# Where a recurrent-memory transformer kernel computes and stores its early values, and how its light and last steps are ordered

## The chip, the cores and the metric

The kernel runs on one core of one Trainium2 chip. The metric is the device time of one execution in microseconds (us). A time shown for a kernel is the median of several executions; a profile is one execution, recorded by the hardware, and its span runs from the first instruction to the last.

A core has five engines with a queue each. TensorE (PE) multiplies matrices, VectorE (DVE), ScalarE (ACT) and GpSimd (POOL) work on elements, and SyncE (SP) computes nothing: here it issues nearly all DMA transfers, one behind the other. An engine works through its own queue in order and waits at an instruction until the semaphores that this instruction needs have been raised.

## What is computed

Four layers are run in turn on a sequence of 2048 tokens of width 512: an attention layer A with a recurrent memory, a dense layer B, then A and B again with the same weights.

```python
def _A_ref(x, mem0, Wq, Wk, Wv, Wo, seg_len):        # seg_len 32, M 8 memory rows, H 32 heads of 128
    mem = mem0
    for s in range(n_seg):                            # 64 segments
        xs = x[:, s * seg_len:(s + 1) * seg_len, :]
        h = concatenate([mem, xs], axis=1)            # 40 rows
        q, k, v = h @ Wq, h @ Wk, h @ Wv              # per head
        p = softmax(where(mask, q k^T * scale, -1e9))
        o = (p @ v) @ Wo
        mem = o[:, :M, :]                             # goes into the next segment
        outs.append(o[:, M:, :])
def _B_ref(x, w1, w2):                                # 512 -> 1376 -> 512
    return relu(x @ w1) @ w2
x = x + _A_ref(layernorm(x), mem0, ...)
x = x + _B_ref(layernorm(x), w1, w2)
x = x + _A_ref(layernorm(x), mem0, ...)
x = x + _B_ref(layernorm(x), w1, w2)
```

Each segment needs the memory that the segment before it produced, so the segments of one layer can't run side by side.

## The kernel before

**Steps.** Time is cut into 68 steps, k = 0 to LAST = 67. Step k works on segment k of the first attention layer and on segment k-4 of the second one, so steps 0 to 3 and 64 to 67 hold one attention layer ("single") and the 60 between them hold two. The chain inside a step is: queries and keys of 16 heads (`qk`, matmuls in `qk_batch`, L528), `scores` (L562), `softmax`, the same for the other 16 heads, transposed probabilities (`transpose_p`, L604), `weighted_v` (L630), `output_mem` (L570) for the memory rows, `new_memory` (L763, casts at L757, L774, L777), and `memory_values` (L711), the values of the new memory rows. The rest is put between as filler for PE: the outputs of the step before (`block`, `output_x`, L364/L387/L392), the dense layer (`dense_h`, L464; `dense_y`, L487), values of the second layer (L345) and values of the first layer that don't hang on the memory (`values0`, L304).

**Order.** For PE, DVE, SP and POOL the order in which the code is written is the order of the queue. ACT's order is chosen by the scheduler when the program is built.

**Values of the first layer.** A group is `values0(p, n)`: the 64 tokens of segments 2p and 2p+1 times 1024 columns of Wv, eight 128x512 matmuls; ACT casts the result into an SBUF buffer, and two DMAs store it into a DRAM tile `vd0[p]`, from which the step that needs it loads its rows (`load_values`). Only odd p go this way, four groups each. Step 0 computes eight groups, step 1 four, and then every fourth step, 5, 9, ..., up to 61, a few (`values_at`): three in steps 5 to 33, four in steps 37 to 61. A step with three is called light (`split`), and so is step 1; in it the dense layer's first product comes after the second scores, in a step with four before them.

**Buffers.** In step 0 the cast values stand in the space of w1 and w2 (`slots`), which are loaded only in step 1 (`load_dense`). Later they stand in one of five buffers named `vst`, which the values of the memory (`VmS`) and a copy of the new memory (`wm`) use too.

**Loading and SP's queue.** At the start SP issues the loads of Wq, Wk, Wv (two halves each) and Wo (four pieces, L148), 16 MB in all, then the stores of step 0 as their casts come, then in step 1: the load of 128 rows of x (`load_xb`), the values of segment 1 (L685), the two stores of the memory's values (L716), their two loads (L721), w1 and w2 in three DMAs (L156, L157, L159), and the stores of step 1's groups (L312). Step 2 follows on the same queue: stores of its memory values, `Vs` of segment 2 (L693), the transpose of the normalized rows by DMA (`transpose_step`, L287, into `xnT`, which `dense_h` reads), the loads L721 and the transpose of the probabilities (L611). SP's DMAs take eight semaphores in turn, so each DMA also waits until the DMA eight places earlier has landed.

**Inputs.** `xbs[n]` holds 128 rows of x, which are normalized and transposed into `xT0[n]` (`inputs_T`): by PE for n < 3, by DMA from n = 3 on, in step 3 for n = 3. Groups with p = 2n and 2n+1 read it.

**The last step.** Step 67 divides the outputs of step 66 over its waits in pieces of 8, 8 and 16 heads (`part`, `block`). Behind it stand `output_x(LAST)`, whose products are summed in two halves by head (`by_heads`), the sums into the residual (`add_output`, L408), a layer norm, a transpose and the last dense layer.

Of the kernel before, what the change touches and what calls it, by code (L numbers as in the profile page):

```python
# [7 lines left out]
BF = mybir.dt.bfloat16  # L8
# [14 lines left out]
def kernel(  # L23
# [14 lines left out]
    nc = tc.nc  # L38
# [92 lines left out]
    hh = H // 4  # L131
# [102 lines left out]
    def transpose_pe(xn):  # L234
        tp = ps_fill.tile([128, NC4, 128], BF, tag="fill", name="tpx")
        for c4 in range(NC4):
            nc.tensor.transpose(tp[:, c4, :], xn[:, c4 * 128:(c4 + 1) * 128], ident[:])
        return tp

    def inputs_T(n):  # L240
        xT0[n] = wk.tile([128, NC4, 128], BF, tag="xT0", bufs=3, name="xT0")
        if n < 3:
            tp = transpose_pe(xbs.pop(n))
            nc.scalar.copy(out=xT0[n][:], in_=tp[:])
        else:
            nc.sync.dma_start_transpose(out=xT0[n][:], in_=xbs.pop(n)[:])

# [41 lines left out]

    def values0(p, n, lo=0, hi=NC4, pool=None, stage=None):
        r = 64 * (p % 2)
        if (n, lo) == (0, 0):
            vd0[p] = dram.tile([64, H * Dh], BF, tag="vd0", bufs=3, name="vd0")
        if lo == 0:
            pool, tag = (pool, "wo") if pool else (ps_fill, "fill")
            vp_tiles[p, n] = pool.tile([128, 512], F32, tag=tag, name="vp")  # L300
        vp = vp_tiles[p, n]
        for c4 in range(lo, hi):
            for j in range(2):
                nc.tensor.matmul(vp[64 * j:64 * j + 64, :], lhsT=xT0[p // 2][:, c4, r:r + 64],  # L304
                                 rhs=Wv_sb[:, c4, (n + j) * 512:(n + j + 1) * 512],
                                 start=(c4 == 0), stop=(c4 == NC4 - 1), tile_position=(0, 64 * j))
        if hi < NC4:
            return
        vst = wk.tile([128, 512], BF, tag="vst", bufs=5, name="vst")[:] if stage is None else stage
        nc.scalar.copy(out=vst, in_=vp[:])  # L310
        for j in range(2):
            nc.sync.dma_start(out=vd0[p][:, (n + j) * 512:(n + j + 1) * 512], in_=vst[64 * j:64 * j + 64, :])  # L312

    def values_first(ii):

# [130 lines left out]

    def dense_h(d):
        if not 0 <= d <= LAST:  # L450
            return
        lo, hi = span(d)
        n = hi - lo

        def cols(c4):
            return xnT_tiles[d + 2][:, c4, lo:hi]

        hT = hT_tiles[d] = wk.tile([128, NFC, 64], BF, tag="hT", bufs=1, name="hT")
        for f0, f1 in ((8, NFC), (0, 4), (4, 8)) if d == LAST - 1 else ((8, NFC), (0, 8)):
            hp = ps_fill.tile([128, 8, 64], F32, tag="fill", name="hp")  # L460
            for fc in range(f0, f1):
                fs = 128 if fc < NFC - 1 else F_LAST
                for c4 in range(NC4):
                    nc.tensor.matmul(hp[0:fs, fc - f0, 0:n], lhsT=w1_sb[:, c4, fc * 128:fc * 128 + fs],  # L464
                                     rhs=cols(c4), start=(c4 == 0), stop=(c4 == NC4 - 1))
# [236 lines left out]
    def memory_values(k, stage=(None, None), part=range(2)):  # L702
        if 0 in part:
            vmds[k] = dram.tile([2, 4, 32, 512], BF, tag="vmd", bufs=7, name="vmd")
        vmd = vmds[k]
        for ii in part:
            vp = ps_c.tile([128, 512], F32, tag="c", name="vm")
            for c4 in range(NC4):
                for j in range(4):
                    n = 4 * ii + j  # L710
                    nc.tensor.matmul(vp[32 * j:32 * j + 32, :], lhsT=HTm[:, c4, :],  # L711
                                     rhs=Wv_sb[:, c4, n * 512:(n + 1) * 512],
                                     start=(c4 == 0), stop=(c4 == NC4 - 1), tile_position=(0, 32 * j))
            VmS = wk.tile([128, 512], BF, tag="vst", bufs=5, name="VmS")[:] if stage[ii] is None else stage[ii]
            nc.scalar.copy(out=VmS, in_=vp[:])  # L715
            nc.sync.dma_start(out=vmd[ii].rearrange("j t e -> (j t) e"), in_=VmS)  # L716

    def load_memory_values(k, act):
        for ii in range(2):
# [6 lines left out]
    def block(k, lo, hi):  # L726
        output_x(k - 1, lo, hi)
        groups = values_at(k)
        if split(k):

            rest = [(i, 0, NC4) for i in range(1, len(groups))]
            todo = [(0, 0, 2)] if lo == 0 else [(0, 2, NC4)] if hi == 16 else rest
        else:
            todo = [(i, c4, c4 + 2) for i in range(len(groups)) for c4 in range(0, NC4, 2)
                    if lo < 8 * i + 2 * c4 + 2 <= hi]
        for i, c_lo, c_hi in todo:
            p, n = groups[i]
            values0(p, n, c_lo, c_hi, ps_wo if i in (0, 2 if len(groups) == 3 else 3) else None)

    def split(k):  # L740
        return k == 1 or len(values_at(k)) == 3

    def values_at(k):


        if k == 1:
            return [(5, 4), (5, 6), (3, 4), (3, 6)]
        if k % 4 != 1 or not has0(k + 1):
            return []
        groups = [(p, n) for p in range(7, NSEG // 2, 2) for n in range(0, NCH, 2)]  # L750
        i = k // 4 - 1
        lo = 3 * min(i, 8) + 4 * max(i - 8, 0)
        return groups[lo:lo + (3 if i < 8 else 4)]

# [35 lines left out]
    def first_step():  # L790


        slots = iter([w1_flat[:, 512 * i:512 * i + 512] for i in range(NC4 * Dff // 512)] +
                     [w2_flat[:, 512 * i:512 * i + 512] for i in range(4)])
        masks(0)
        with tc.high_priority(offset=PRIO):
            qks = qk(0, [0])
# [34 lines left out]
    def step(k):  # L832
# [68 lines left out]
        if k == 1:  # L901
            normalize(nc.vector, xbs[n_x], xbs[n_x], moments_x(n_x), 0, 128)
        if single and k < LAST and ahead:
            add_dense(k - 2)
            store(k - 2)
# [31 lines left out]
    with tc.manual_schedule(engines={mybir.EngineType.PE, mybir.EngineType.DVE, mybir.EngineType.SP,  # L937
# [79 lines left out]
```

## Time and profile before

| | |
|---|---|
| median of 3 executions | 1606.83 us (1605.47 to 1611.45) |
| the profiled execution, its own time | 1606.83 us |
| its span | 1605.1 us |
| PE busy | 1568.9 us, 98% of the span, 42714 instructions |
| DVE busy | 1264.7 us, 79% |
| ACT busy | 738.8 us, 46% |
| POOL busy | 346.6 us, 22% |
| mean granted TensorE clock | 0.996 |
| DMA traffic of SP's queue | 136.10 MB, 37.9% of 16 engines' span |

The profile names lines as L12, tiles as out<-in, and has several views. A timeline row is: start, duration, engine, line, operation, tiles, size, count, and in square brackets the idle time of the engine just before with what ended it. SPq is SP's queue: the time that it took to issue a DMA, not the time of the transfer. A row of the windows view gives the length of a stretch, busy time and instruction count of each engine, PEclk (the clock that was granted to TensorE, 1.00 is full), the mean busy share of the DMA engines, and GB/s.

### The profile page before, as it was taken

How to read it: one execution, taken by the hardware profiler on the slowest of the kernel's cores; microseconds unless marked ns; L12 is line 12 of the kernel's file. 1: busy time of each engine (PE TensorE's matmuls, PEld its weight loads, DVE VectorE, ACT ScalarE, POOL GpSimd, SP SyncE). 2: the span in 40 equal slices, each digit the busy share in tenths (PEclk: the TensorE clock that was granted, in tenths of full speed). 3: DMA queues.
4: the chain of work that ended last, by engine and by line, in shares of the span. 5: the costliest groups of instructions: out<-in, count | busy, mean ns of one | idle time of the engine just before them, and what ended most of it. 6: DMA issues, size and time to landing. Idle time of an engine off the chain costs nothing.

```text
span 1605.1 us, 94862 instructions
## 1 busy us (share of the span) xinstructions
PE 1568.9 (98%) x42714; PEld 1322.8 (82%) x42714; DVE 1264.7 (79%) x3112; ACT 738.8 (46%) x1799; POOL 346.6 (22%) x666
## 2 busy tenths in 40 slices
PE   5899999999999999999999999999999999999997
PEld 3577888888888888889888887988888898888876
DVE  4478888888888887888888888888888888787865
ACT  3334445444544544454454445445454544545432
POOL 2012222222222222222222222222222222221210
PEclk9999999999999999999999999999999999999999
DMA  9733343343343434434443443343343333334222
GB/s 369 222 83 77 75 87 89 64 97 85 78 76 90 87 63 97 84 72 83 84 92 63 100 85 74 84 84 91 68 100 82 77 77 79 92 61 100 69 70 36
DMA packets 216373, 146.39 MB, mean 91 GB/s; under 512 B 124984, under 2 KB 209312, under 8 KB 214944
## 3 DMA queue, kind: packets, MB, share of 16 engines
q1 hardware_dynamic: 212816, 136.10, 37.9%
q8 instruction: 335, 5.49, 1.5%
q0 software_dynamic: 3072, 4.20, 1.1%
q14 instruction: 70, 0.57, 0.1%
q10 hardware_dynamic: 80, 0.03, 0.0%
HBM read 65.41 MB, written 45.35 MB: 69 GB/s over the span
## 4 chain that ended last, share of the span: by engine, by line
PE 91%; DVE 4%; SPq 2%; issue 1%; DMA 1%; ACT 1%; POOLq 0%; POOL 0%; ACTq 0%; DVEq 0%
PE qp L528 35%; PE wox L364 10%; PE wo L570 8%; PE vm L711 7%; PE v L345 7%; PE hp L464 6%; PE sp L487 5%; PE sp L562 4%; PE pv L630 4%; PE vp L304 3%; SPq L148 1%; PE tp L604 1%; PE xp L438 1%; DMA Wo_sb<-in_A_Wo_dram 1%; SPq L134 1%
## 5 line engine op out<-in xcount | busy, mean ns | idle before, releaser
L534 ACT CAST QT<-qp 128x480 bf16<-128x480 f32 (+3 forms) x408 | 201.1, 493 | 396.0 <-PE qp L528 395.6
L528 PE MATMUL qp<-HT,Wk_sb 128*128 128x80 bf16 (+1 forms) x8704 | 369.7, 200 | 2.7 <-issue 0.9
L528 PE MATMUL qp<-HT,Wq_sb 128*128 128x80 bf16 (+1 forms) x8704 | 370.4, 200 | 1.8 <-POOL HT L700 1.2
L528 PEld LDWEIGHTS <-Wq_sb 128*128 128x128 bf16 x8704 | 326.6, 100 | 33.6 <-issue 26.3
L528 PEld LDWEIGHTS <-Wk_sb 128*128 128x128 bf16 x8704 | 329.0, 100 | 4.5 <-issue 2.9
L536 DVE CAST KT<-qp 128x480 bf16<-128x480 f32 (+3 forms) x408 | 225.1, 565 | 104.1 <-PE qp L528 101.8
L594 POOL TENSOR_TENSOR P_sb<-es,sm 128x320 bf16<-128x320 f32 x185 | 130.5, 719 | 752.9 <-ACT es L584 491.6
L578 DVE TENSOR_REDUCE mx<-sp 128x8 f32<-128x320 f32 x256 | 115.7, 487 | 75.1 <-PE sp L562 73.4
L364 PE MATMUL wox<-Wo_sb,OTx 128*64 128x256 bf16 x2880 | 173.9, 273 | 0.1
L364 PEld LDWEIGHTS <-OTx 128*64 128x64 bf16 x2880 | 150.2, 110 | 3.2 <-issue 0.2
L589 DVE TENSOR_REDUCE sm<-es 128x8 f32<-128x320 f32 x256 | 118.6, 463 | 42.3 <-ACT es L584 32.8
L711 PE MATMUL vm<-Wv_sb,HTm 128*32 128x512 bf16 x2176 | 136.4, 380 | 0.8 <-DVE HT L777 0.8
L584 ACT ACTIVATE es<-es 128x320 f32<-128x320 f32 x256 | 110.2, 469 | 54.2 <-DVE es L582 52.9
L570 PE MATMUL wo<-Wo_sb,OTm 128*32 128x512 bf16 x2144 | 128.7, 381 | 3.4 <-DMA Wo_sb<-in_A_Wo_dram 3.3
L345 PE MATMUL v<-Wv_sb,xnT 128*32 128x512 bf16 x2048 | 129.2, 378 | 0.0
L554 DVE CAST sp<-maskb 128x320 f32<-128x320 bf16 x256 | 118.3, 484 | 0.0
L582 DVE TENSOR_TENSOR es<-sp,mx 128x320 f32<-128x320 f32 x256 | 113.7, 483 | 1.6
L711 PEld LDWEIGHTS <-HTm 128*32 128x32 bf16 x2176 | 89.5, 96 | 28.9 <-issue 11.5
L487 PE MATMUL sp<-w_sb,hT 128*64 128x256 bf16 (+4 forms) x1474 | 105.3, 276 | 0.5 <-ACT hT L470 0.5
L715 ACT CAST VmS<-vm 128x512 bf16<-128x512 f32 x134 | 78.4, 585 | 54.4 <-PE vm L711 54.4
L464 PE MATMUL hp<-xnT,w_sb 128*128 128x64 bf16 (+3 forms) x2948 | 100.5, 193 | 0.5 <-ACT xnT L973 0.4
L464 PEld LDWEIGHTS <-w_sb 128*128 128x128 bf16 (+1 forms) x2948 | 94.3, 101 | 1.5 <-issue 1.1
(113 smaller groups left out, 2027.2 us busy)
## 6 DMA issues: line engine op xcount, KB each, us to landing
Vs<-vd SPq DMA_DIRECT2D x96, 256.0 KB
vmd<-VmS SPq DMA_DIRECT2D x134, 128.0 KB
vd<-vst SPq DMA_DIRECT2D x128, 128.0 KB
Vs<-vmd SPq DMA_DIRECT2D x254, 32.0 KB
Vs<-vmd SPq DMA_DIRECT2D x60, 128.0 KB
vd<-vst SPq DMA_DIRECT2D x112, 64.0 KB
Wq_sb<-in_A_Wq_dram SPq DMA_DIRECT2D x2, 2048.0 KB
Wk_sb<-in_A_Wk_dram SPq DMA_DIRECT2D x2, 2048.0 KB
```

The costliest lines, as they stand in the source:

```text
L345: nc.tensor.matmul(vp[32 * j:32 * j + 32, :], lhsT=tokens[:, c4, :], rhs=Wv_sb[:, c4, n * 512:(n + 1) * 512], start=(c4 == 0), stop=(c4 == ...
L364: nc.tensor.matmul(out[64 * j:64 * j + nr, 0:256], lhsT=lhsT, rhs=rhs[:, 256 * j:256 * j + 256], start=start, stop=stop, tile_position=(0, ...
L464: nc.tensor.matmul(hp[0:fs, fc - f0, 0:n], lhsT=w1_sb[:, c4, fc * 128:fc * 128 + fs], rhs=cols(c4), start=(c4 == 0), stop=(c4 == NC4 - 1))
L487: nc.tensor.matmul(sp_banks[bank][64 * j:64 * j + n, 0:w], lhsT=hT_tiles[d][0:fs, fc, 0:n], rhs=w2_flat[0:fs, fc * Dm + 256 * j:fc * Dm + ...
L528: nc.tensor.matmul(qp[:, hi, 0:ncol], lhsT=W_sb[:, c4, h * Dh:(h + 1) * Dh], rhs=HT[:, c4, a_lo:a_hi, :], start=(c4 == 0), stop=(c4 == NC4 ...
L534: nc.scalar.copy(out=dst[:, 0:nh, a_lo * L:a_hi * L], in_=qp[:, 0:nh, 0:ncol])
L536: nc.vector.tensor_copy(out=dst[:, 0:nh, a_lo * L:a_hi * L], in_=qp[:, 0:nh, 0:ncol])
L554: nc.vector.tensor_copy(out=sp_tiles[a], in_=maskb2)
L570: nc.tensor.matmul(wo[32 * j:32 * j + 32, :], lhsT=OTm[:, h, n, 2 * M * c:2 * M * c + 4 * M], rhs=Wo_sb[:, h, :], start=(h < 4), stop=(h > ...
L589: nc.vector.tensor_reduce(out=sm[:], in_=es[:], axis=AX.X, op=ALU.add)
L594: eng.tensor_tensor(out=P, in0=es[:], in1=sm[:].unsqueeze(2).to_broadcast([128, 8, L]), op=ALU.mult)
L711: nc.tensor.matmul(vp[32 * j:32 * j + 32, :], lhsT=HTm[:, c4, :], rhs=Wv_sb[:, c4, n * 512:(n + 1) * 512], start=(c4 == 0), stop=(c4 == NC ...
```

## The change

Six things are changed.

1. Step 0 computes eleven groups instead of eight (also (3, 4), (3, 6) and (5, 4)), between five pieces of Wo instead of four: 8, 8, 8, 4 and 4 heads. Step 1 has three groups instead of four, step 5 two instead of three, step 37 three instead of four; all other steps keep their number, with the groups moved up.
2. The stores of step 0 that come from `values0` and `memory_values` are not issued in step 0. They are kept in a list (`held`) and issued in step 1 behind `load_memory_values`, ahead of `load_dense`: 24 DMAs. The two stores of `values_second` stay where they were.
3. Rows 384 to 511 of x (n = 3) are loaded behind Wo into a `vst` buffer, which they keep until step 3, normalized in step 1 behind the first batch of queries and keys (before: near the end of step 1), and transposed by PE into an extra copy in the buffer `ob`, from which step 1 computes (7, 0) and (7, 2). The transpose by DMA in step 3 stays.
4. In light steps the first of `dense_h`'s two pieces (12 of 44 matmuls) goes ahead of the second scores. Steps with two or three groups are light; so step 37 becomes light, and 61 and the others with four do not.
5. The last step divides the outputs of step 66 into 4, 4 and 24 heads and puts that same piece of `dense_h` ahead of the last 24.
6. `output_x(LAST)` is summed by quarters of 128 columns instead of two halves of 256 columns by head: 128 matmuls instead of 64, and four sums of 32x128 instead of 32x256.

```diff
 def load_xb(n):
-        tag, bufs = ("vst", 5) if n in (1, 2) else ("xb", 1)
+        tag, bufs = ("vst", 5) if n in (1, 2, 3) else ("xb", 1)
...
+    WO_PARTS = ((0, 8), (8, 16), (16, 24), (24, 28), (28, 32))
...
-        for pc in range(4):
-            nc.sync.dma_start(out=Wo_sb[:, pc * hh:(pc + 1) * hh, :], in_=Wo_v[:, pc * hh:(pc + 1) * hh, :])
+        for h0, h1 in WO_PARTS:
+            nc.sync.dma_start(out=Wo_sb[:, h0:h1, :], in_=Wo_v[:, h0:h1, :])
+        load_xb(3)
...
-    def inputs_T(n):
-        xT0[n] = wk.tile([128, NC4, 128], BF, tag="xT0", bufs=3, name="xT0")
-        if n < 3:
-            tp = transpose_pe(xbs.pop(n))
+    def inputs_T(n, early=False):
+        tag, bufs = ("ob", 1) if early else ("xT0", 3)
+        xT0[n] = wk.tile([128, NC4, 128], BF, tag=tag, bufs=bufs, name="xT0")
+        if n < 3 or early:
+            tp = transpose_pe(xbs[n])
...
+    held = []
+
+    def put(later, **store):
+        if later:
+            held.append(store)
+        else:
+            nc.sync.dma_start(**store)
...
         for j in range(2):
-            nc.sync.dma_start(out=vd0[p][:, (n + j) * 512:(n + j + 1) * 512], in_=vst[64 * j:64 * j + 64, :])
+            put(stage is not None, out=vd0[p][:, (n + j) * 512:(n + j + 1) * 512], in_=vst[64 * j:64 * j + 64, :])
...
     def by_heads(k):
-        return k == LAST or k + 1 < LAST and len(layers(k + 1)) == 1
+        return k + 1 < LAST and len(layers(k + 1)) == 1
...
-    def dense_h(d):
+    def dense_h(d, parts=slice(None)):
...
+        pieces = ((8, NFC), (0, 4), (4, 8)) if d == LAST - 1 else ((8, NFC), (0, 8))
+        for f0, f1 in pieces[parts]:
...
-            nc.sync.dma_start(out=vmd[ii].rearrange("j t e -> (j t) e"), in_=VmS)
+            put(k == 0, out=vmd[ii].rearrange("j t e -> (j t) e"), in_=VmS)
...
     def split(k):
-        return k == 1 or len(values_at(k)) == 3
+        return len(values_at(k)) in (2, 3)
...
-        if k == 1:
-            return [(5, 4), (5, 6), (3, 4), (3, 6)]
+        if k in (1, 5):
+            return [(5, 6), (7, 0), (7, 2)] if k == 1 else [(7, 4), (7, 6)]
...
             wo = ps_wo.tile([128, Dm], F32, tag="wo", name="wo")
-            for i in range(4):
-                if i < 2:
-                    values0(1, 4 + 2 * i, stage=next(slots))
-                output_mem(0, wo, 8 * i, 8 * i + 8)
+            for groups, heads in zip((((1, 4),), ((1, 6),), ((3, 4),), ((3, 6), (5, 4)), ()), WO_PARTS):
+                for p, n in groups:
+                    values0(p, n, stage=next(slots))
+                output_mem(0, wo, *heads)
...
-        if has_x and (k % 4 == 0 or k == 1):
+        if k % 4 == 0 and has_x:
             load_xb(n_x)
         with tc.high_priority(offset=PRIO):
-            qks = qk(0, act, behind=norm_rows.pop(k, None))
+            behind = norm_rows.pop(k, None)
+            if k == 1:
+                def behind():
+                    normalize(nc.vector, xbs[n_x], xbs[n_x], moments_x(n_x), 0, 128)
+            qks = qk(0, act, behind=behind)
             load_values(k, act)
             if k == 1:
                 memory_values(k)
-        part = 8 if single else 5
+                inputs_T(n_x, True)
+        part = 4 if k == LAST else 8 if single else 5
+        mid = 8 if k == LAST else 16
...
             load_memory_values(k, act)
+            while held:
+                put(False, **held.pop(0))
             scores(qks, act)
...
         if single:
-            block(k, part, 16)
+            block(k, part, mid)
         elif light:
+            dense_h(k - 2, slice(0, 1))
             block(k, part, 16)
...
         if single:
-            if k < LAST:
-                dense_h(k - 2)
-            block(k, 16, H)
+            dense_h(k - 2, slice(0, 1) if k == LAST else slice(None))
+            block(k, mid, H)
         elif light:
-            dense_h(k - 2)
+            dense_h(k - 2, slice(1, None))
             block(k, 16, H)
...
         output_x(LAST, 0, H)
-        dense_h(LAST - 2)
+        dense_h(LAST - 2, slice(1, None))
         add_output(LAST)
```

More of the change, by code (lines that the diff above doesn't have):

```diff
@@ L130 @@
     PW = H * Dh // 2
-    hh = H // 4
+    WO_PARTS = ((0, 8), (8, 16), (16, 24), (24, 28), (28, 32))
     def load_w(W_sb, W_v, pc):
@@ L238, in transpose_pe @@
         return tp
-    def inputs_T(n):
-        xT0[n] = wk.tile([128, NC4, 128], BF, tag="xT0", bufs=3, name="xT0")
-        if n < 3:
-            tp = transpose_pe(xbs.pop(n))
+    def inputs_T(n, early=False):
[3 more added lines that the diff above has]
+            tp = transpose_pe(xbs[n])
             nc.scalar.copy(out=xT0[n][:], in_=tp[:])
         else:
-            nc.sync.dma_start_transpose(out=xT0[n][:], in_=xbs.pop(n)[:])
+            nc.sync.dma_start_transpose(out=xT0[n][:], in_=xbs[n][:])
     def norm_parts(k):
@@ L456, in cols @@
             return xnT_tiles[d + 2][:, c4, lo:hi]
-        hT = hT_tiles[d] = wk.tile([128, NFC, 64], BF, tag="hT", bufs=1, name="hT")
-        for f0, f1 in ((8, NFC), (0, 4), (4, 8)) if d == LAST - 1 else ((8, NFC), (0, 8)):
+        if not parts.start:
+            hT_tiles[d] = wk.tile([128, NFC, 64], BF, tag="hT", bufs=1, name="hT")
+        hT = hT_tiles[d]
+        pieces = ((8, NFC), (0, 4), (4, 8)) if d == LAST - 1 else ((8, NFC), (0, 8))
+        for f0, f1 in pieces[parts]:
             hp = ps_fill.tile([128, 8, 64], F32, tag="fill", name="hp")
@@ L731, in block @@
             rest = [(i, 0, NC4) for i in range(1, len(groups))]
-            todo = [(0, 0, 2)] if lo == 0 else [(0, 2, NC4)] if hi == 16 else rest
+            if k == 1:
+                todo = [] if lo == 0 else [(0, 0, 2)] if hi == 16 else [(0, 2, NC4)] + rest
+            else:
+                todo = [(0, 0, 2)] if lo == 0 else [(0, 2, NC4)] if hi == 16 else rest
         else:
@@ L737, in block @@
             p, n = groups[i]
-            values0(p, n, c_lo, c_hi, ps_wo if i in (0, 2 if len(groups) == 3 else 3) else None)
+            values0(p, n, c_lo, c_hi, ps_wo if i in (0, 3 if len(groups) == 4 else 2) else None)
     def split(k):
-        return k == 1 or len(values_at(k)) == 3
+        return len(values_at(k)) in (2, 3)
     def values_at(k):
-        if k == 1:
-            return [(5, 4), (5, 6), (3, 4), (3, 6)]
+        if k in (1, 5):
+            return [(5, 6), (7, 0), (7, 2)] if k == 1 else [(7, 4), (7, 6)]
         if k % 4 != 1 or not has0(k + 1):
             return []
-        groups = [(p, n) for p in range(7, NSEG // 2, 2) for n in range(0, NCH, 2)]
-        i = k // 4 - 1
+        groups = [(p, n) for p in range(9, NSEG // 2, 2) for n in range(0, NCH, 2)]
+        i = k // 4 - 2
         lo = 3 * min(i, 8) + 4 * max(i - 8, 0)
@@ L793, in first_step @@
         slots = iter([w1_flat[:, 512 * i:512 * i + 512] for i in range(NC4 * Dff // 512)] +
-                     [w2_flat[:, 512 * i:512 * i + 512] for i in range(4)])
+                     [w2_flat[:, 512 * i:512 * i + 512] for i in range(8)])
         masks(0)
@@ L839, in step @@
         ahead = has1(k + 1) or not cont
-        if has_x and (k % 4 == 0 or k == 1):
+        if k % 4 == 0 and has_x:
             load_xb(n_x)
         with tc.high_priority(offset=PRIO):
-            qks = qk(0, act, behind=norm_rows.pop(k, None))
+            behind = norm_rows.pop(k, None)
+            if k == 1:
+                def behind():
+                    normalize(nc.vector, xbs[n_x], xbs[n_x], moments_x(n_x), 0, 128)
+            qks = qk(0, act, behind=behind)
             load_values(k, act)
@@ L900, in step @@
             outputs(k, pvs)
-        if k == 1:
-            normalize(nc.vector, xbs[n_x], xbs[n_x], moments_x(n_x), 0, 128)
         if single and k < LAST and ahead:
```

## The prediction

> **What bounds the kernel now.** I read the chain of work that ended last first, then PE's timeline step by step, then SP's queue around steps 0 to 2, then the granted clock. The chain is PE's:
>
> ```profile
> PE 91%; DVE 4%; SPq 2%; issue 1%; DMA 1%; ACT 1%; POOLq 0%; POOL 0%; ACTq 0%; DVEq 0%
> ```
>
> A matmul removed from a full step therefore saves its time, and a late PE is late to the end, because each step needs the memory of the step before. What is left to win lies where PE waits: step 0 (the loads of Wo), a short wait in each light step, and the last step. PE's timeline shows the three.
>
> ```profile
> 49.76 0.79 PE L570 MATMUL wo<-Wo_sb,OTm 128*32 128x512 bf16 x8 [2.15 <-DMA Wo_sb<-in_A_Wo_dram]
> ...
> 82.24 1.34 PE L464 MATMUL hp<-xnT,w_sb 128*128 128x32 bf16 x44
> ...
> 239.23 0.42 PE L562 MATMUL sp<-KT,QT 128*40 128x40 bf16 x16
> 239.83 0.37 PE L562 MATMUL sp<-KT,QT 128*40 128x40 bf16 x16 [0.18 <-DVE sp L554]
> 240.14 1.52 PE L464 MATMUL hp<-xnT,w_sb 128*128 128x64 bf16 x44
> ...
> 1587.92 0.48 PE L604 MATMUL tp<-ident,P_sb 128*64 128x80 bf16 x16 [1.60 <-DVE P_sb L594]
> ...
> 1589.45 3.59 PE L387 MATMUL wox<-Wo_sb,OTx 128*32 128x256 bf16 x64
> ```
>
> The reader should see that the last quarter of Wo's products waits 2.15 us, and that 82.24 is where step 2 first needs w1 and `xnT`: no wait stands before it. The windows view adds the clock:
>
> ```profile
> 47.00:50.00 3.00, 0.85 (x16) 0.33 (x15) 0.00 (x0) 0.00 (x0) 0.00 (x0) 1.00 0.83 274
> 50.00:53.00 3.00, 2.21 (x54) 1.16 (x47) 1.20 (x3) 0.77 (x2) 0.00 (x0) 0.51 0.39 98
> ...
> 1586.10:1589.50 3.40, 1.69 (x70) 1.36 (x60) 2.62 (x7) 1.23 (x3) 0.00 (x0) 1.00 0.00 0
> 1589.50:1592.90 3.40, 3.40 (x64) 2.38 (x64) 1.34 (x5) 0.14 (x1) 0.00 (x0) 0.50 0.02 5
> ```
>
> After each of the two thinly used stretches TensorE is granted half its clock. Last, SP's queue, which I take to decide this change:
>
> ```profile
> 44.31 10.59 SPq L312 DMA_DIRECT2D vd<-w_sb  x12
> ...
> 56.13 2.83 SPq L312 DMA_DIRECT2D vd<-w_sb  x4
> ...
> 60.20 0.89 SPq L716 DMA_DIRECT2D vmd<-VmS  x2
> 63.08 0.67 SPq L721 DMA_DIRECT2D Vs<-vmd  x2
> 63.80 0.40 SPq L156 DMA_DIRECT2D w_sb<-in_B_w_dram  x1
> ...
> 67.40 9.24 SPq L312 DMA_DIRECT2D vd<-vst  x8
> 76.77 1.01 SPq L716 DMA_DIRECT2D vmd<-VmS  x2
> 78.29 0.33 SPq L693 DMA_DIRECT2D Vs<-vd  x1
> 78.73 2.21 SPq L287 DMA_TRANSPOSE xnT<-XN  x1
> ```
>
> Issuing the stores costs SP 0.88 us each while Wo still loads, 0.71 after it (2.83/4). From w1's issue at 63.80 to the product that needs `xnT` at 82.24 the queue has no slack: the transpose is issued until 80.94 and lands near 82.2.
>
> **Step 0 and the start of step 1.** The three added groups fill the waits for Wo. At about 1.0 us each (eight L304 matmuls took 1.05 at 44.23) PE is busy until about 49.4 and Wo lands, as now, at 49.7: the stores stood behind it on the queue already, so their leaving frees little. The last piece is 4 heads, not 8: about 0.35 (half of the 0.62 that eight took at 47.00) instead of 0.79, a gain of 0.5. With PE filled the clock should stay full: step 1's first queries and keys took 4.38 (52.05 to 56.43) against 3.44 in step 3 (91.98 to 95.42), and the memory's values 2.05 against 1.84; gain 1.15. Against it, normalizing 128 rows on DVE behind the first key cast: rows of 0.68, 0.18, 0.15, POOL 0.56 and 0.41, about 2.1 us with gaps, in front of the second key cast, whose PSUM bank the second half of the memory's values needs; I charge 0.3 (0 to 1.1). The four transposes (0.40 at 27.51) replace four L304 matmuls (0.5). The softmax's chain, not the filler, ends the second half (P_sb done at 66.66, PE at 66.72), so the group removed there gains nothing. PE would reach step 2 some 1.5 us earlier.
>
> **The stores moved into step 1.** This is where I expect the loss. Between the loads L721 and w1 now stand 24 stores: 2 of 128 KB and 22 of 64 KB. The last L721 is issued when the memory's second store has landed: the cast now ends at 59.19, would end at 59.19 - 1.65 + 0.3 = 57.8, and the row from 60.66 (second store) to 63.46 (its load) gives at most 2.8, so SP is free for them at about 60.6. In step 5 four such stores took 2.46 (0.62 each), here 0.71; I take 0.65: 22 x 0.65 + 2 x 0.45 = 15.2. So w1 is issued at 75.8, not 63.80. The price has bounds: 0.38 from the shortest issue nearby (L693, 0.33 and a gap), 0.88 from the row of twelve; that is 69.7 to 81.7.
>
> What is late next, in rows of before, counted from w1's issue: w2 also has to wait for the last stores (its space held their values), but its data goes behind w1's, so that wait hides. The queue first stands still for w2's landing at 74.94, 11.1 after w1's issue; the cast of the memory's second half, whose buffer is one of the `vst` stored behind w2, starts at 75.83, 12.0 after. In the changed queue the two stores of step 2's memory values hang on just these: 12.0 + 0.6 cast + 0.45 store + 0.4 L693 + 1.2 to 2.2 for the transpose + 1.25 landing = 16.5. So `xnT` arrives at 75.8 + 16.5 = 92.3, where PE needs it at about 80.7 and had it at 82.24: 10.0 later than before. Nothing else of PE's can go ahead, since its order is fixed. Behind a wait of 11 us the clock will be at half for one or two stretches of 3.4 us; the small products lose little (1.15 over the 6.4 us of step 1), the wide ones nearly half (L387 3.53 us against 32 in 0.99, so 1.98 for 64, in step 2), so 1.0 to 3.0, taken as 1.9. Step 3 then starts 11.9 us late (bounds 5.0 to 19.0). The gains of steps 0 and 1 are inside this sum: they only bring the first store forward.
>
> **Light steps.** The two halves of the second scores take 0.91 (239.23 to 240.14) where step 37 needs 0.42, since the mask of the second layer is written late. The piece of `dense_h` put ahead (12 of 44 matmuls, 0.40) covers that; ACT's changed order puts a cast of 0.58 between the two exponentials, which takes back about 0.1. Net 0.4 in each of steps 9, 13, ..., 33: 2.8. Step 5 loses a group as well (0.92), but the probabilities are ready at 150.22 where PE arrives at 150.96, so 0.5. Step 37 becomes light: 23.45 now, against 23.09 - 0.4 in its like, 0.75.
>
> **The last step.** More filler in the wait of 1.60 should keep the clock full: `output_x` 128 matmuls at 0.0156 (64 in 1.00 at 1585.25) are 2.0 instead of 3.53, less 0.1 for late operands: 1.45. Four sums of 32x128 (1.15 at 1589.72) instead of 1.76: 0.6. Less filler ahead of the scores: 0.1. Sum 2.15; without the clock 0.7.
>
> [...]
>
> **Sum.** 1605.1 + 11.9 - 2.8 - 0.5 - 0.75 - 2.15 = 1610.8 us of span. The profiled execution took 1.7 us more than its span, and is itself the median of the runs shown: 1612.5 us, 0.35% more.
>
> **Rivals.** (a) *The stores are hidden.* SP would have to issue them so fast that `xnT` meets PE at 80.7: w1 by 64.2, 24 issues in 3.6 us. Then 1605.1 - 1.5 - 6.2 + 1.7 = 1599.1. For it: the transfers themselves (1.6 MB) are small, and the DMA engines are 0.34 to 0.57 busy from 50 to 62. Against: no issue on the page is under 0.3. (b) *Slower for certain: SP pays the dear price.* If a store costs 0.88 as from 44.31, w1 is issued at 81.7 and step 3 starts 19 late: 1619.6. It decides from 0.75 on: then the kernel is over 1614.9. For it: two of the thirteen issues from 49.74 to 58.96 took over a microsecond. Against: the twelve were slowed by Wo. (c) *The change doesn't do what it says*: the hole comes, but the light steps gain nothing, because ACT's order delays the second exponential, and the last step's clock drops all the same: 1612.5 + 2.8 + 1.45 = 1616.8. For it: only 0.2 us lie between the probabilities and PE in light steps.
>
> **Numbers.** The forecast (with its own bounds on the cheap side, down to 1605) has 0.50, (a) 0.14, (b) 0.24, (c) 0.12. 0.5% (8.0 us, about what a measurement of this kernel can tell from no change) puts the limits at 1598.8 and 1614.9. (a) lies on the lower limit, with 0.10 beyond it; the forecast gives 0.04 to slower, (c) half: faster 0.10, same 0.56, slower 0.34. The range, 1602 to 1620, leaves out (a) and what is beyond (b).
>
> **What would show it.** In the profile after: w1's issue at 74 to 78; a wait of about 10 us before the first L464-type product of step 2, put down to the transpose or to w1, with PEclk near 0.5 behind it; PEclk 1.00 from 50 to 56; no idle before the scores in light steps; the last step's outputs in about 2.0. No such wait, or w1's issue before 70, makes the prediction wrong.

## The result and the profile after

The changed kernel takes 1616.61 us (median of 6 executions, 1615.67 to 1619.7), the kernel before 1606.54 us beside it (6 executions). The ratio is 1.0061, 95% interval 1.0044 to 1.0077: slower by 0.61%, some 10 us. The profiled execution after took 1616.37 us, its span is 1614.7 us, so 9.6 us above the span before.

PE's timeline after shows the places that the prediction spoke of: the end of step 0, the first product of step 2 that needs `xnT`, a light step (9), and the last step. Lines of the changed kernel stand lower in its file: L477 was L464, L402 was L387, L734 was L721, L157 was L156.

```profile
49.23 0.62 PE L583 MATMUL wo<-Wo_sb,OTm 128*32 128x512 bf16 x8
...
80.75 0.38 PE L575 MATMUL sp<-KT,QT 128*40 128x40 bf16 x16
95.09 1.55 PE L477 MATMUL hp<-xnT,w_sb 128*128 128x32 bf16 x44 [13.96 <-DMA xnT<-XN]
...
253.39 0.58 PE L477 MATMUL hp<-xnT,w_sb 128*128 128x64 bf16 x12
253.90 0.62 PE L314 MATMUL vp<-Wv_sb,xT 128*64 128x512 bf16 x4
254.36 0.56 PE L575 MATMUL sp<-KT,QT 128*40 128x40 bf16 x32
...
1597.92 0.48 PE L617 MATMUL tp<-ident,P_sb 128*64 128x80 bf16 x16 [0.58 <-DVE P_sb L607]
...
1600.20 1.62 PE L402 MATMUL wox<-Wo_sb,OTx 128*32 128x128 bf16 x101
1602.69 0.57 PE L402 MATMUL wox<-Wo_sb,OTx 128*32 128x128 bf16 x27 [0.87 <-issue]
```

The three waits shown of before are gone or shorter: none before the last piece of Wo (2.15), none between the scores in step 9 (0.18), 0.58 in place of 1.60 before the last transposes. In their place stands one new wait of 13.96 us, before L477 in step 2. SP's queue says why:

```profile
58.55 0.83 SPq L734 DMA_DIRECT2D Vs<-vmd  x2
59.44 0.34 SPq L302 DMA_DIRECT2D vmd<-w_sb  x1
59.83 9.18 SPq L302 DMA_DIRECT2D vd<-w_sb  x12
69.05 0.59 SPq L302 DMA_DIRECT2D vmd<-w_sb  x1
69.68 8.18 SPq L302 DMA_DIRECT2D vd<-w_sb  x10
77.91 0.59 SPq L157 DMA_DIRECT2D w_sb<-in_B_w_dram  x1
...
91.69 1.31 SPq L289 DMA_TRANSPOSE xnT<-XN  x1
```

The 24 held stores fill the queue from 59.44 to 77.86; then comes w1 (L157), which was issued at 63.80 before, and 13.8 us behind it the transpose. The windows view of the same execution shows the clock:

```profile
47.00:50.00 3.00, 2.84 (x32) 1.03 (x24) 0.00 (x0) 1.78 (x4) 0.00 (x0) 1.00 0.63 208
50.00:53.00 3.00, 2.15 (x83) 1.85 (x84) 1.43 (x4) 1.02 (x3) 0.00 (x0) 1.00 0.28 90
80.00:85.00 5.00, 1.13 (x43) 0.78 (x39) 2.56 (x7) 0.48 (x2) 0.46 (x2) 0.79 1.01 362
...
95.00:100.00 5.00, 4.91 (x94) 3.94 (x93) 0.00 (x0) 0.69 (x3) 0.00 (x0) 0.51 0.27 62
```

With step 0 filled the clock stays full from 47 to 53 (0.51 from 50 to 53 before). It is lost within the new wait, and is still at half when L477 starts. From 80 to 85 the DMA engines are fully busy: w1 and w2 are being moved while PE stands still.

Where the 9.6 us came from can be read from the start of `mt`, the first product of each step's `new_memory`, taken here as the end of a step. Step 1 ends 1.95 earlier than before (68.94 for 70.89); step 2 ends at 104.13 (89.45 before), 14.68 late; step 66's `mt` is 11.32 late; the end is 9.6 late. So step 2 alone costs 16.6 us, of which steps 0 and 1 had won 2.0 beforehand; 3.4 are won in the steps between, and 1.7 in the last step.

### The profile page after: what moved, and what is told of

Read it like the earlier page. It is cut to its first block, busy times and chain, and to the rows that moved or that the text cites. A ratio compares the mean times of both kernels' runs of the same rounds, so it can differ in the third digit from the quotient of the medians.

```text
span 1614.7 us, 94984 instructions
## 1 busy us (share of the span) xinstructions
PE 1568.4 (97%) x42782; PEld 1323.0 (82%) x42782; DVE 1262.5 (78%) x3112; ACT 738.0 (46%) x1800; POOL 346.7 (21%) x666
## 4 chain that ended last, share of the span: by engine, by line
PE 94%; DMA 2%; DVE 1%; SPq 1%; ACT 1%; issue 1%; POOLq 0%; ACTq 0%; DVEq 0%
PE qp L541 37%; PE wox L374 10%; PE wo L583 8%; PE vm L724 7%; PE v L355 7%; PE hp L477 6%; PE sp L500 5%; PE pv L643 4%; PE sp L575 4%; PE vp L314 3%; DMA Wv_sb<-in_A_Wv_dram 2%; PE tp L617 1%; PE xp L448 1%; PE wox L397 1%; DMA vd<-vst 0%
## 5 line engine op out<-in xcount | busy, mean ns | idle before, releaser
L583 PE MATMUL wo<-Wo_sb,OTm 128*32 128x512 bf16 x2144 | 128.9, 380 | 0.4 <-issue 0.4
L477 PE MATMUL hp<-xnT,w_sb 128*128 128x64 bf16 (+3 forms) x2948 | 102.7, 193 | 14.4 <-DMA xnT<-XN 14.0
L477 PEld LDWEIGHTS <-w_sb 128*128 128x128 bf16 (+1 forms) x2948 | 95.5, 101 | 15.4 <-issue 9.8
```

The costliest lines, as they stand in the source:

```text
L583: nc.tensor.matmul(wo[32 * j:32 * j + 32, :], lhsT=OTm[:, h, n, 2 * M * c:2 * M * c + 4 * M], rhs=Wo_sb[:, h, :], start=(h < 4), stop=(h > ...
```

## The experiments

All kernels but the last-step one are built on the changed kernel. Ratios are to the kernel before, run beside each on the same chip. "w1" is when SP issued it, "hp" PE's wait before L477 in step 2, "step 2" the time when it ends.

| kernel | stores | w1 | hp | step 2 | span | ratio, 95% interval |
|---|---|---|---|---|---|---|
| before | 18, SP in step 0 | 63.80 | 0 | 89.45 | 1605.1 | 1 |
| after | 24 held, SP | 77.91 | 13.96 | 104.13 | 1614.7 | 1.0061, 1.0044 to 1.0077 |
| e3_xb_own | 24 held, SP, own buffer | 78.29 | 14.71 | 103.18 | 1614.2 | 1.0064, 1.0047 to 1.0080 |
| e2_hold_ten | 10 held, SP | 70.38 | 3.73 | 97.19 | 1609.7 | 1.0030, 1.0019 to 1.0041 |
| e1_no_hold | 24, SP in step 0 | 69.27 | 0 | 96.83 | 1606.8 | 1.0016, 1.0005 to 1.0027 |
| e4_pool_stores | 24 held, POOL | 63.83 | 0 | 95.47 | 1608.0 | 1.0024, 1.0012 to 1.0035 |
| e9_pool_held_xb | 24 held, POOL, own buffer | 64.76 | 3.21 | 95.50 | 1608.0 | 1.0027, 1.0014 to 1.0041 |
| e7_pool_step0 | 24, POOL in step 0 | 63.49 | 0 | 92.54 | 1604.1 | 0.9997, 0.9987 to 1.0006 |
| e8_pool_step0_xb | 24, POOL in step 0, own buffer | 63.61 | 0 | 92.44 | 1602.9 | 0.9995, 0.9985 to 1.0006 |
| e10_ten_pool | 14 SP in step 0, 10 held, POOL | 65.10 | 0 | 90.64 | 1604.5 | 0.9984, 0.9973 to 0.9995 |
| e11_fourteen_pool | 10 SP in step 0, 14 held, POOL | 61.46 | 0 | 89.84 | 1602.3 | 0.9985, 0.9972 to 0.9997 |

### None held, ten held

```diff
     def put(later, **store):
-        if later:
+        if False:
```

> The changed kernel with every store of step 0 issued as its cast comes, none held for step 1. Theory (the 24 held stores stand ahead of w1 on SP's queue at about 0.79 us each, and everything behind them is late by that): SP is then free for w1 at about 67 to 69 us instead of 77.9, xnT of step 2 lands near 82 to 85, and the wait of PE before hp in step 2 falls from 13.96 us to 0 to 5 us; in exchange the loads of step 1's memory values come late, and weighted_v of step 1 waits up to 5 us. Time 1603 to 1609 us. Rival (the extra work of step 0, or the buffers, make the hole, whichever step the stores are issued in): the wait before hp stays over 10 us and the time stays at 1614 or more.

```diff
-            put(stage is not None, out=vd0[p]...
+            put(hold, out=vd0[p]...
-            put(k == 0, out=vmd[ii]...
+            put(False, out=vmd[ii]...
```

Here `hold` is true for the five groups between the pieces of Wo only.

> The changed kernel with ten stores held instead of 24 (those of the five groups between the Wo pieces); the other fourteen are issued in step 0. Theory (SP's queue, about 0.79 us per held store): w1 is issued some 14 x 0.79 = 11 us earlier, at 67 to 69 us, the wait before hp in step 2 is 3 to 6 us instead of 13.96, and the time is about 1606, 1604 to 1609. Rival (a hole that does not scale with the number of held stores): the wait before hp stays over 10 us, 1614 or more.

With none held, the wait before L477 is gone, and the price appears where the theory put it. In PE's timeline of that kernel:

```profile
64.97 0.48 PE L617 MATMUL tp<-ident,P_sb 128*64 128x80 bf16 x16 [0.60 <-DVE P_sb L607]
70.64 0.69 PE L643 MATMUL pv<-PT,Vs 40*128 40x40 bf16 x16 [5.20 <-DMA Vs<-vmd]
71.16 0.70 PE L643 MATMUL pv<-PT_sb,Vs 40*128 40x40 bf16 x16
71.79 3.61 PE L583 MATMUL wo<-Wo_sb,OTm 128*32 128x512 bf16 x32
```

The memory's values of step 1 (L734) are loaded late, because SP is busy with the stores of step 0 until 64.8; PE waits 5.20, and L583 then takes 3.61 where it takes 1.91 at full clock. The time is 1608.69, inside 1603 to 1609. With ten held, the stores take 7.04 us of the queue, w1 goes at 70.38 (67 to 69 expected), and the wait is 3.73:

```profile
87.66 1.55 PE L477 MATMUL hp<-xnT,w_sb 128*128 128x32 bf16 x44 [3.73 <-DMA xnT<-XN]
```

The time is 1610.3, a little above the expected 1604 to 1609: PE also stood 1.34 us for "issue" in step 2. Waits of 0, 3.73 and 13.96 for 0, 10 and 24 stores: the rival (step 0's work or the buffers, whatever SP does) falls.

### Buffers or queue

```diff
-        tag, bufs = ("vst", 5) if n in (1, 2, 3) else ("xb", 1)
+        tag, bufs = ("vst", 5) if n in (1, 2) else ("xb", 1)
```

> The changed kernel with x block 3 in a buffer of its own, so that it takes none of the five buffers which the value stores of step 1 share. Theory (SP's queue sets the hole): the cast of the second half of the memory's values and xnT of step 2 come at most 1.2 us earlier, the wait before hp stays at 12.5 us or more, time 1615 to 1617. Rival (the shortage of buffers sets it): most of the hole goes, the wait before hp is under 5 us, about 1603 to 1606.

In the chain of waits after, the piece before `xnT` is a cast on ACT that waits 7.34 us for a `vst` store to land, so a shortage of buffers was a fair suspect. With a buffer more that wait is gone from ACT, and the chain of this kernel reads:

```profile
77.64 2.20 DMA vd<-w_sb
...
79.92 9.55 DMA w_sb<-in_B_w_dram
...
89.53 0.34 SPq L302
...
90.95 3.64 DMA xnT<-XN
...
94.64 1.55 PE hp L477 x44
```

w2 waits for the last held store to land (its space held those values), takes 9.55 us behind w1, and only when it has landed does SP's queue go on to the store at 89.53 and the transpose. `xnT` comes 0.45 us earlier, no more. The two waits end at nearly the same time (90.06 after, 89.47 here), behind the transfers of w1 and w2, so removing one of them shows the other; the queue is the cause.

### The same stores from POOL

```diff
             if k == 1:
+                while held:
+                    nc.gpsimd.dma_start(**held.pop(0))
                 memory_values(k)
...
-            while held:
-                put(False, **held.pop(0))
```

> The changed kernel with its 24 held stores issued from POOL's queue, behind the second normalization of step 1, in place of SP's. Theory (SP's queue sets the hole): w1 is issued at 62 to 66 us, xnT of step 2 lands before or up to 2 us after PE needs it, the wait before hp falls from 13.96 us to 2 or less, and the time is 1600 to 1605. Rival (the 24 transfers themselves, or the lanes on which each transfer waits for an earlier one, make w1 and w2 late whichever queue issues them): the wait before hp stays over 8 us, 1611 or more.

w1 goes at 63.83 and the wait before L477 is gone, but 1608.46 us is above what the theory gave, and the rival's wait before L477 does not come either. The stall has moved. ACT's timeline:

```profile
72.30 0.36 ACT L547 CAST QT<-qp 128x240 bf16<-128x240 f32 x1 [0.91 <-PE qp L541]
80.06 0.59 ACT L728 CAST VmS<-vm 128x512 bf16<-128x512 f32 x1 [7.39 <-DMA vd<-vst]
```

POOL issues a store every 0.52 us until 67.37; w2 still has to wait for the last of them and is issued at 72.88, and the `vst` stores and the cast at 80.06 stand behind it. ACT's next casts of QT are queued behind that cast, and PE waits 6.57 us in the queries:

```profile
80.69 0.69 PE L541 MATMUL qp<-HT,Wq_sb 128*128 128x40 bf16 x16 [6.57 <-ACT VmS L728]
```

Three runs followed: the same with the buffer of its own, and the stores from POOL in step 0 with none held (in `put`: `nc.gpsimd.dma_start(**store)` in place of `held.append(store)`), with and without that buffer.

> The 24 stores held for step 1 and issued from POOL's queue, as in the first run of that kind, and x block 3 in a buffer of its own. There ACT stood 7.39 us before the cast of the memory's second half and PE 6.57. Theory (that wait was for a buffer whose store stood behind w2; w2 itself waits for the last stores from its space, until about 73): the wait in step 2's queries goes, but xnT still comes behind w2's landing at about 79, so PE waits 2 to 5 us before hp; time 1603 to 1607. Rival (only the buffer was in the way): no wait over 1 us, 1598 to 1602.

> The changed kernel with the 24 stores issued from POOL's queue in step 0 as their casts come; none is held and SP issues none of them. Theory (the loss is w1 and w2 behind the held stores; POOL is nearly idle from 42 to 54 us): w1 is issued on SP at 59 to 62 us, w2 within 2 us of it, PE waits 1 us or less before hp in step 2, no wait for the memory's values in step 1, steps 1 and 2 take about 18.4 and 18.6 us, time 1597 to 1602. Rival (the 1.7 MB of stores beside the load of Wo, or POOL's small operations behind the stores, cost as much as the hole): PE waits for Wo, or for POOL in step 1, in all 4 us or more, time 1603 or more.

> As the last one, with x block 3 also in a buffer of its own. Theory (with w1 and w2 early the five shared buffers come free in time): within 1 us of the last one. Rival (the buffers are a second limit of their own): 1.5 us or more below it, and a wait of ACT before the cast of the memory's second half in the last one that is gone here.

With the buffer, the held stores from POOL leave 3.21 us before L477, as expected, but another stop of 3.56 us put down to "issue" brings the time to 1609.67, above the expected 1607. Without holding, the hole of step 2 is gone and step 0 ends 3.8 us later (54.33 for 50.53). POOL's timeline shows the rival's second half at work:

```profile
25.72 0.58 POOL L300 DMA_DIRECT2D vmd<-w_sb  x1 [8.77 <-ACT w_sb L728]
28.22 2.09 POOL L300 DMA_DIRECT2D vd<-w_sb  x4 [1.92 <-ACT w_sb L320]
30.32 0.58 POOL L222 TENSOR_TENSOR rstd<-rstd,mhalf_t 128x1 f32<-128x1 f32 x1
```

The small operation at 30.32, which is at 27.07 after, stands behind stores that wait for ACT's casts. VectorE's normalization of x block 2 waits 3.73 for it, and PE 3.23, with the clock at half for the 3.41 us from 31.94 on. POOL was nearly idle, yet not free to wait. The expected 1597 to 1602 was wrong: 1605.96 and, with the buffer, 1604.59, 1.4 us apart, which their scatter does not tell from none. ACT's wait of 1.10 us for a buffer in the first is gone in the second, but no wait of PE in step 2 hangs on it in either: with w1 early the buffer is no second limit that these runs can show.

### Divided between the queues

The last ten stores go to POOL behind its normalization of step 1, the other fourteen to SP in step 0 behind the loads of Wo (the edits of the runs with ten held and with POOL together); then fourteen and ten.

> The changed kernel with fourteen stores issued by SP in step 0, behind the loads of Wo, and the last ten held for step 1 and issued from POOL. Theory (two prices decide: each store ahead of w1 on SP costs about 0.75 us, and each store that reaches the DMA engines before Wo has landed delays Wo): step 0's end stays at 50.4 to 50.6, w1 is issued at 62.5 to 64, w2 at most 2 us later, PE waits 1.5 us or less for data in step 2 (a stop for instructions may add up to 1.5), step 2 is done by 90; span 1599 to 1602, ratio to before 0.996 to 0.999. Rival (the stores cost what they cost, wherever they go): 4 us or more of waits in steps 0 to 2, ratio 1.000 or more.

> As the last one, with fourteen stores held for POOL and ten issued by SP in step 0. Theory (SP's queue sets w1's issue): SP is free about 4 x 0.8 = 3 us earlier, w1 is issued at 60 to 62, and w2 follows once POOL's last store has landed, at 64 to 66; xnT is there when PE needs it; time within 1 us of the last one, at best 1 us below it. Rival (POOL's later stores hold w2 up, as with 24): the wait before hp grows to 2 us or more.

Both are faster than the kernel before, by 0.16% and 0.15%, with intervals that lie below 1, and 0.76% faster than the changed one. SP's queue of the second:

```profile
59.83 1.41 SPq L734 DMA_DIRECT2D Vs<-vmd  x2
61.46 0.40 SPq L157 DMA_DIRECT2D w_sb<-in_B_w_dram  x1
67.76 0.40 SPq L158 DMA_DIRECT2D w_sb<-in_B_w_dram  x1
...
76.54 1.31 SPq L289 DMA_TRANSPOSE xnT<-XN  x1
```

`xnT` is there before PE needs it. Yet step 2 takes 20.7 us in both, where it took 18.56 in the profile before and 19.8 in another with the same steps 0 to 2 (the last-step run below): PE stops 1.90 and 1.69 us in it for "issue", time for which the profile shows no releaser. With ten on POOL the ratio is as expected, but nearly every part came out later: step 0 ends at 51.16 (50.6 at most expected), w1 goes at 65.10 (64), step 2 ends at 90.64 (90), the span is 1604.5 (1602). With fourteen, w2 at 67.76 is later than the 64 to 66 expected, held by POOL's last stores, but without harm. The gain is smaller than its parts promise, and the two runs below, which keep one or the other division and change only the light steps, have 0.9991 (0.9979 to 1.0003) and 1.0005 (0.9993 to 1.0018). The first three of these four ratios go by the same 29 executions of the kernel before, so they are not independent. The division undoes the loss for certain; whether it wins a tenth of a percent over the kernel before stays open.

### The last step alone

The kernel before, with the change of the last step only (4, 4 and 24 heads, the piece of `dense_h` ahead, quarters).

> The kernel before with the change of the last step alone (4, 4 and 24 heads among its waits, the dense piece ahead, sums in quarters). Forecast's term: 2.15 us less, 1.45 of it by the clock. By the trace of the changed kernel 1.7. Expected: the granted clock 1.00 to the end, the wait before the last transposition 0.6 or less in place of 1.60, the last step (from its mt to the end) 1.4 to 2.2 us shorter, time 1603 to 1606. Rival (the clock stays full only because step 0's hole moved the windows of the clock): a stretch at half clock after the wait, gain 0.8 or less.

From `mt` of step 66 to the end it took 30.49 us (32.72 before, 31.0 after): 2.2 less, with PEclk 1.00 until 1598 in this profile, so the rival's reason (step 0's hole) falls; the wait before the last transposes is 0.67. But the median is 1605.88 for 1605.43 before, ratio 1.0002 (0.9991 to 1.0012): the gain does not show in the time, and the profiled execution was the fastest of ten. Twelve other profiles with this last step take 30.2 to 32.3 us in it. In the kernel with fourteen stores on POOL the clock was lost after all:

```profile
1586.25 0.33 PE L643 MATMUL pv<-PT,Vs 40*128 40x40 bf16 x7 [0.61 <-issue]
...
1587.23 3.74 PE L402 MATMUL wox<-Wo_sb,OTx 128*32 128x128 bf16 x128
```

### Light steps

Two edits on the divided kernels. With ten on POOL, the piece of `dense_h` between the two layers' scores:

```diff
-            dense_h(k - 2, slice(0, 1))
             block(k, part, 16)
...
-            scores(qks, act)
+            scores(qks, act, (lambda: dense_h(k - 2, slice(0, 1))) if light and not single else None)
```

> As the run with ten stores on POOL, and in the light steps the piece of dense_h stands between the scores of the two layers in place of ahead of both. Theory (ahead of both, the piece makes the first layer's scores and so the softmax's first maximum 0.4 us later, and the softmax's chain, not PE, then ends last before the transposes; between them the first scores come as early as in the kernel before): the light steps 9, 17, 21, 25, 33 take 22.65 to 22.85 us in place of 22.95 (23.09 before). Rival (the statistics on VectorE ahead of the cast of PT_sb are what is left): 22.90 to 23.00, no change. On the whole time 1 to 2.5 us, within the scatter of the runs.

The light steps take 23.03 us where PE doesn't stop (23.03 to 23.17 in the five): neither the theory nor the rival. PE's timeline of step 9:

```profile
240.83 0.42 PE L577 MATMUL sp<-KT,QT 128*40 128x40 bf16 x16
241.19 0.59 PE L477 MATMUL hp<-xnT,w_sb 128*128 128x64 bf16 x12
241.70 0.37 PE L577 MATMUL sp<-KT,QT 128*40 128x40 bf16 x16
```

PE has no gap, and arrives at the transposes at 245.81, when the probabilities have been ready since 245.64. So here PE is the limit: divided, scores, piece and four L314 products take 1.63 us (240.38 to 242.01), together 1.46 (253.39 to 254.85 after).

With fourteen on POOL, the statistics of the next x block moved (`mom["x"] = moments_x(n_x)` goes from the light step to before the second scores of the full step behind it):

> The kernel with fourteen stores on POOL, and the statistics of the next x block (0.69, 0.18 and 0.15 us on VectorE) taken out of the light steps, where they stand ahead of the cast of PT_sb, and put into the full step behind each, where VectorE waits 0.77 us for the scores. Theory (of the 0.42 us that the piece ahead wins in a light step, 0.17 goes to the wait for P_sb and 0.11 to this cast): light steps 9, 17, 21, 25, 33 take 22.80 to 22.88 us in place of 22.95, and steps 10, 18, 22 stay at 23.38. Rivals: the chain to P_sb alone decides, light steps 22.95; or the statistics are as dear in the full step, and steps 10, 18, 22 grow by 0.1 to 0.3. On the whole at most 1 us, so ratio to before 0.997 to 0.999, within the scatter of the kernel with fourteen stores.

Light steps take 22.99, and PE waits 0.12 for the probabilities in them; steps 10, 18 and 22 take 23.51 in place of 23.38. Both rivals hold: the chain to P_sb decides in light steps, and the statistics are no cheaper in the full step. The ratio, 1.0005, is above the 0.997 to 0.999 expected.

## Why the prediction came out as it did

The mechanism was right: the hole in step 2, its place, its cause and the clock behind it. The size was short by 3.9 us (span 1610.8 forecast, 1614.7 measured): 2.8 at the start of step 3, 0.7 in the steps between, 0.4 in the last one. That was enough to take the kernel over the 0.5% that I called same, so "slower", with 0.34, came in place of "same", with 0.56. The median is within 0.2 us of rival (c)'s 1616.8, but that is luck: (c) had a smaller hole and a last step without its clock. By its steps:

- **Stores ahead of w1: the term that was mis-sized.** I said 15.2 us of issues from 60.6, w1 at 75.8. Measured: from 59.44, 18.4 us, w1 at 77.91. The 22 stores of 64 KB cost 0.79 each (9.18 and 8.18 over 22), not 0.65. Eighteen of them were issued in 0.45 to 0.68 us, as I had taken from step 5; four took 1.52, 1.14, 1.78 and 1.37. Step 5's four stores held no long one; the row of four before, 0.71 each, did. The mean of a few issues was taken for a price where four of 22 cost over 1 us. Rival (b) was said to decide from 0.75, and that is where it came out, though not at its 0.88. I took the twelve stores behind that 0.88 for slowed by Wo. In fact their 10.59 us hold a time in which SP issued nothing and waited for Wo's landing, from 48.08 to 49.74:

```profile
SPq L312 <- DMA Wo_sb<-in_A_Wo_dram: 1.6, 1, 1.6
```

Without it the twelve cost 0.74 each, long ones included, much nearer to what was measured than my 0.65.

- **From w1's issue to `xnT`:** 16.5 forecast, 17.2 measured; both waits that I named, for w2's landing and for the cast, are in the traces, and the run with its own buffer showed that the first is enough by itself. PE arrived at 81.1 (80.7 said). L477 starts 12.85 later than before (10.0 said).
- **Clock behind the hole:** step 3 starts 14.68 late, 1.8 more than L477, against 1.9.
- **Step 0 and step 1:** right. No wait for Wo, clock 1.00, step 0 0.70 shorter (0.5 said), step 1 in 18.41 us (19.66 before).
- **Light steps: wrong in size.** 0.4 said; 22.95 for 23.09, so 0.14, in the steps 9, 17, 21, 25 and 33, where neither profile has a stop. PE does come 0.42 earlier to the large L314 block (15.80 after the step's start for 16.22). But both kernels finish the second scores at 14.83, so the softmax ends no earlier, and now PE arrives with it: the transposes start only 0.25 earlier. I had read 0.91 for two halves as waste; the wait in it was 0.18, and no more was to be had: the two edits show PE on one side (23.03) and the softmax on the other (22.95 to 22.99).
- **Steps 5 and 37:** step 37 gained 0.49 (0.75 said). Step 5 lost 0.25 in this profile (a gain of 0.5 said), with waits of 0.26 and 0.83; in seven of the eleven other profiles with this step 5, those with none and ten held among them, it took 22.90, a gain of 0.35, and in three 23.54 to 23.69. What decides there stays open.
- **The sum of the middle was nearly right for the wrong reason.** From step 5's end to step 63's the profiles have 1358.81 before and 1355.18 after. The kernel with only the last step changed, whose light steps are those of before, has 1355.35. Compared matmul by matmul, some 2.5 of the 3.5 us between these two are stops for "issue" in the one execution.
- **The last step: nearly right in the sum, but not by its terms.** 2.15 said, 1.7 measured. The sums gave the 0.6 said (1.17 for 1.76). The outputs gave 0.53 in place of 1.45: at full clock their 128 matmuls took 3.06 us, not 2.0, with a stop of 0.87 among them. Ten of the thirteen profiles with these quarters have such a stop, of 0.87 to 1.42 us, and took 3.06 to 3.61 for the outputs; the other three had half the clock there, and took 3.43 to 3.75. So the clock that I counted on was worth little here. The rest came from a term put at 0.1: the outputs start 0.57 earlier. The last transposes are 1.32 earlier, less a stop of 0.60 behind them; but 0.73 of the 1.32 is a stop in the profile before, at the scores that those transposes wait for, which none of the thirteen has there:

```profile
1584.72 0.30 PE L562 MATMUL sp<-KT,QT 128*40 128x40 bf16 x10 [0.73 <-issue]
```

Rival (c)'s half about the clock did not happen in this profile, but does in others, so the gain is not to be counted on.

## What to carry to other kernels

Work put off is put ahead of something: before moving DMA issues to a later place, list what is queued behind that place and multiply by a mean price that includes the long issues and leaves out waits, not by the usual one. A resource that looks idle can still not take work that waits: stores on POOL blocked a 0.58 us operation that VectorE and PE needed. Filling a wait is worth the wait that the profile shows, not the time that the products around it seem to take. And narrower products are more instructions: 128 quarters took 3.06 us at full clock where their price elsewhere promised 2.0.

## What the runs showed of the hardware

- **Issues of equal stores on one queue.** On SP most 64 KB stores of step 0 took 0.45 to 0.60 us, and one in four to eleven took 1.0 to 1.8, in each kernel that issued them there (three of 16 before, 1.04 to 1.47; four of 22 after, 1.14 to 1.78); on POOL all took 0.52 to 0.59. The cause of the long ones is open.
- **The clock.** Every stretch at half clock before the last few microseconds is a multiple of 3.41 us long (3.41 and 6.83 before, 17.07 after, 13.65 with none held). The changes of the granted clock lie a whole number of 3.413 us apart: before, those at 50.08, 56.91, 1589.49, 1592.91 and 1603.15 us are 2, 449, 1 and 3 of these apart; after, those at 82.86 and 99.93 are 5 apart. The same last step kept its clock in 8 of 13 profiles, lost it in the outputs in 3 and in the dense product behind them in 2; what decides between these was not shown. PE need not stand still for a drop. In the 3.41 us that end at a change, it was busy for 0.93 and 1.70 us ahead of the first two drops before, for 1.58 ahead of the drop after and for 2.09 with fourteen stores, while other such stretches with 1.97 (before) and 2.08 to 2.40 (after) kept the clock; so the busy time of a stretch doesn't decide alone. In the kernel with fourteen stores:

```profile
1583.80:1587.20 3.40, 2.09 (x89) 1.67 (x76) 2.10 (x6) 0.71 (x2) 0.00 (x0) 0.99 0.00 0
1587.20:1590.60 3.40, 3.28 (x117) 3.02 (x121) 1.37 (x5) 0.19 (x1) 0.00 (x0) 0.50 0.02 5
```

- **Two queues.** With ten stores moved from SP to POOL, w1 was issued at 65.10 in place of 70.38, and the wait of 3.73 us before L477 was gone: SP's time for issuing was what the hole was made of.
- **Stops for "issue".** The profile names no releaser for them, but its DMA records bear on them. Its page of before has this queue:

```profile
q8 instruction: 335, 5.49, 1.5%
```

These are 335 packets of 16 KB, for 42714 matmuls and as many weight loads: 255 instructions of PE to a packet, if PE's are all that they carry. In the 14 profiles there are 71 such stops of over 0.3 us behind 50 us, and every one of them ended 1.0 to 1.7 us after a packet of this queue had landed (1.08 to 1.56 for the three before, 1.29 to 1.41 for the four after); of moments taken at random 15% lie so. The DMA engines were full ahead of some (busy share 1.07 from 75 to 80 with ten held) and idle in others (0.02 from 1601.8 to 1605.2 after). That PE was waiting for its own instructions is an estimate from these counts; no run changed their number to test it. Packets never started less than 3.2 us apart (3.23 before, 3.34 after), and 128 quarters with their weight loads are 256 instructions, which fits the 3.06 us and more that they took. Some stops recur at one place (the last outputs in ten of thirteen profiles, the outputs of step 4 in eleven of 14, 0.32 before and 0.60 after), others don't. Steps 6 to 63 of the 14 profiles vary from 1354.8 to 1358.8 us, in good part by them; they are why single microseconds can't be told apart in the time of this kernel.
